# A gated linear attention and a routed expert layer in one kernel: a later start of the emptied rows, two squares on another engine, one load on another queue, and a new listed order

## The chip, the core and the metric

The kernel runs on one core of a Trainium2 chip. A core has a matrix engine (TensorE, PE in the profile; its weight loads are PEld), a vector engine (VectorE, DVE), a scalar engine for activation functions (ScalarE, ACT), a general engine (GpSimd, POOL) and SyncE (SP), which here only issues DMAs. Each engine runs its own instructions in the order in which the program lists them, and waits at an instruction until what it needs is there. SBUF is the on-chip memory, PSUM the eight banks into which TensorE writes, HBM the memory outside. The metric is the device time of one execution in microseconds (us); lower is better. All arithmetic is in float32 apart from small counting matrices.

## The reference

```python
# q, k, v, a_re, a_im: (4, 8, 768, 48)
mag = np.sqrt(a_re * a_re + a_im * a_im)
scale = np.minimum(mag, 0.999) / (mag + 1e-06)
a_re_n, a_im_n = (a_re * scale, a_im * scale)
for t in range(S):
    ar, ai = (a_re_n[:, :, t, :, None], a_im_n[:, :, t, :, None])
    new_re = ar * S_re - ai * S_im
    new_im = ar * S_im + ai * S_re
    kv = np.einsum('bhd,bhe->bhde', k[:, :, t], v[:, :, t])
    S_re, S_im = (new_re + kv, new_im)
    y[:, :, t] = np.einsum('bhd,bhde->bhe', q[:, :, t], S_re)
# bridge: x is (3072, 384)
logits = x @ w_gate                      # 8 experts
expert_idx = np.argmax(logits, axis=1)
probs = softmax(logits); gate_w = probs[arange(N), expert_idx]
for e in range(E):
    mask = expert_idx == e
    h = np.maximum(x[mask] @ w1[e], 0.0)     # 384 -> 1024
    out[mask] = gate_w[mask, None] * (h @ w2[e])
```

So there is an attention whose state decays and turns by a complex gate at each of 768 steps, and behind it a layer in which every one of 3072 tokens goes to the one of 8 experts that its router prefers. On the given inputs the experts receive 421, 406, 403, 392, 388, 370, 354 and 338 tokens.

## The kernel before

**Two stages.** In the first stage the attention is computed from the gates' logarithms and angles. It is cut into ten *units* (`UNITS`) of one batch and 128, 256 or 384 time steps; the first two units have 128 and 256 steps. For each unit `front(u)` does the elementwise work, on tiles of 128 partitions by 3 x T. In its order: ScalarE takes Ln of the real part `a` and its reciprocal by Exp (`c`); the imaginary part is multiplied by `c` (L213, on VectorE for unit 0 and on GpSimd for all others); ScalarE squares this (L334), squares the square into `junk` with a running sum (L382), and takes Ln(1 + c); VectorE adds half of it to `a` (L385); ScalarE takes an Exp with a small offset; VectorE cuts `a` at a maximum (L389) and makes three running sums `D` of it (L391, a scan from SBUF); ScalarE takes Exp(D) and Exp(-D), with which q (on GpSimd, on VectorE in unit 0) and k are multiplied (L213). For the angle, ScalarE takes an Arctan, VectorE three running sums `si` (L402, a scan with one operand in PSUM) and three instructions that bring the angle into one turn (L407, L408, L410), ScalarE a sine and a cosine. Four products (L213, into `hz` and `zp`) give q and k turned. DMAs (L429) bring these from the layout by partition into the layout by head.

Ln and Exp are in one table of ScalarE, Arctan and Sin in another, so ScalarE loads a table (L691) at each change between them.

`chunk(b, c)` then does 128 steps of one batch on TensorE: a transpose of k (L458), scores (L466), the masked scores times v (L485), the state's part (L478), the new state (L493), and a product with the constant `turn` that puts out 384 values of the token and the router's logits (L501). VectorE masks the scores (`am`, L213). ScalarE copies the other results out of PSUM. `route` finds expert and place of each token and writes its row with an indirect DMA (L560) into `xs_hbm`, which has 480 places for each expert.

**The empty places.** Not all of the 480 places get a token. Before any token is written, three DMAs (L673) write a constant row with the token number 2^20 into the upper places of all experts: from place `MINC` on. The final scatter leaves such rows out. At the end of the router the kernel compares the counts with `MINC` and the capacities (`counts_ok`); if an expert has fewer than `MINC` tokens, a slow path (from L856) does everything again.

**The order.** All work of the first stage is collected as 980 numbered operations (`P.add`), and then issued in the order of a list that is written out in the program, `ORDER`. The list sets the order on every engine and on each DMA queue. Of the numbers, 0 to 45 are `front(0)`, 62 to 107 `front(1)`; 0 and 1 are the two loads of unit 0's gates, 2 and 3 of its k and q, 62 to 65 the same for unit 1; 46 loads the first v. Number 7 is the square of unit 0, 68 and 69 are unit 1's product on GpSimd and its square. The second stage is ordered by a planner inside the program, from its own operations.

**The second stage.** The experts are run one after the other, the fullest first, each as two layers of matmuls (L815 and L834) with the outputs scattered to HBM (L755). Part of the fullest expert, its first 288 places, starts before the last tokens are routed (`early_layer`, L633).

**Setup.** `setup()` loads `wgr`, the router's weights, 28 KB, as the first DMA on SyncE's queue (L640), and GpSimd builds the constant `turn` from it (L648).

Of the kernel before, what the change touches and what calls it, by code (L numbers as in the profile page):

```python
# [15 lines left out]
ACT = mybir.ActivationFunctionType  # L16
# [14 lines left out]
CAP = 480  # L31
# [5 lines left out]
W = XW + 2  # L37
XR = 9
EARLY = 9
FAR = 4096.0  # L40
MINC = 256
ROUTES = [((0, C),)] * (B - 1) + [((0, 3), (3, 5), (5, 6))]
TB = 8
CEN = 42.0
# [6 lines left out]


ORDER = [int(i) for i in (
    "0 1 62 63 2 4 3 5 46 6 64 7 65 8 294 9 185 66 10 11 67 12 14 13 15 16 68 21 23 22 24 17 26 142 25 69 27 28 70 20 141 71 18 72 19 83 30 29 31 33 32 144 "
    "34 73 38 84 36 145 74 35 76 146 45 143 75 37 43 77 44 40 78 86 147 79 85 39 80 87 251 41 42 88 148 81 49 89 149 90 150 82 47 50 53 151 250 92 55 54 91 "
    "51 93 162 56 94 95 99 97 152 96 100 106 163 254 102 107 103 153 255 104 154 108 105 52 156 101 48 98 57 58 155 253 252 157 256 159 164 165 60 158 166 "
    "346 59 167 115 257 160 258 117 168 259 169 109 260 111 271 116 161 131 170 112 171 119 174 345 110 113 175 125 127 261 172 181 182 114 173 348 126 118 "
    "61 184 121 349 262 176 179 265 350 347 264 178 120 129 177 122 263 123 130 183 273 351 267 133 132 137 268 266 274 124 270 128 135 138 180 272 134 352 "
    "389 275 136 458 353 276 139 457 277 354 192 278 190 140 355 194 193 280 186 269 188 279 196 281 208 366 282 187 191 202 189 198 285 283 288 356 286 "
    "204 284 287 203 206 460 461 195 205 292 357 462 291 218 290 359 197 293 360 199 200 289 207 459 358 210 201 209 463 363 214 367 362 219 212 369 220 "  # L60
    "215 365 464 368 211 302 465 370 221 550 361 304 364 466 549 300 303 305 213 371 298 216 372 222 478 373 223 217 301 224 374 467 319 501 375 378 317 "
    "315 318 376 299 333 225 309 316 552 377 226 468 320 313 383 310 306 469 380 227 335 314 382 471 553 381 329 379 325 330 554 472 385 307 388 326 331 "
    "470 308 384 336 555 334 387 321 475 332 386 323 473 551 481 474 341 480 556 477 311 479 557 322 482 228 665 229 392 230 236 312 237 238 476 558 664 "
    "390 239 231 394 393 324 396 483 395 484 337 570 338 397 339 485 391 412 593 559 340 486 406 327 413 407 490 408 487 491 424 342 328 402 573 499 500 "
    "488 668 343 497 498 409 669 410 667 398 489 411 400 403 571 670 494 560 399 495 418 425 401 492 572 344 493 414 419 561 666 671 709 415 562 404 672 "
    "240 563 416 673 422 564 575 417 496 566 674 426 567 506 241 569 242 428 243 574 232 508 233 507 234 565 423 675 521 509 427 235 522 568 708 244 523 "
    "429 763 537 576 245 502 504 685 577 249 676 503 246 579 513 505 524 247 405 580 519 578 248 420 581 514 538 517 421 583 510 584 518 511 587 533 582 "
    "585 529 586 712 687 297 713 430 591 688 534 714 592 512 539 588 520 431 589 686 525 530 715 590 540 526 711 716 690 527 296 717 545 689 691 528 535 "
    "692 295 678 541 839 729 536 710 693 515 432 677 546 542 433 516 543 434 435 694 443 531 885 444 679 596 544 445 449 532 718 602 597 598 680 682 603 "
    "594 719 547 683 681 446 695 612 595 548 697 610 599 600 611 720 436 841 606 437 684 438 601 613 614 607 604 447 615 448 450 616 439 605 440 721 838 "  # L70
    "622 696 617 618 700 623 441 699 723 442 842 620 451 702 843 698 619 701 628 621 452 722 706 626 629 707 725 844 724 704 731 630 726 728 705 627 608 "
    "845 703 732 846 840 632 730 456 609 631 847 727 624 752 633 453 848 625 734 634 455 733 735 859 768 736 454 770 769 738 783 771 784 764 739 785 737 "
    "740 765 799 766 786 745 775 742 743 849 746 767 635 779 744 800 636 801 741 776 780 781 861 748 753 860 795 749 782 791 796 750 850 853 747 797 792 "
    "637 638 751 644 639 645 646 807 851 852 650 855 647 640 641 862 772 856 858 651 773 648 863 649 658 642 774 864 890 643 857 654 886 891 787 865 887 "
    "866 656 789 802 808 902 798 892 653 659 660 663 888 867 661 893 903 657 906 871 868 898 662 907 872 655 754 869 880 788 870 878 777 652 790 889 876 "
    "803 854 778 874 804 873 882 899 793 881 875 805 794 914 879 806 755 809 756 758 894 810 877 811 895 812 915 757 813 819 904 820 884 821 825 908 759 "
    "905 814 815 822 909 896 883 823 826 938 897 816 817 824 818 762 900 829 760 761 910 901 939 828 912 911 827 936 913 916 937 830 917 940 831 832 918 "
    "919 920 941 926 921 927 942 928 922 923 929 943 932 924 833 925 930 944 931 933 935 834 835 836 945 837 946 934 947 948 954 969 949 955 956 950 951 "
    "952 960 953 957 970 963 961 958 975 964 959 962 965 976 971 966 967 972 979 977 968 973 978 974 "
).split()]  # L80


# [117 lines left out]
def gateloop_then_moe(ctx, tc, gates, qk, v, wg, w1, w2, out):  # L200
# [8 lines left out]
    def bc(ap, shape):  # L209
        return ap.to_broadcast(shape)  # L210
# [83 lines left out]
    with ExitStack() as att:  # L294
# [55 lines left out]
        def front(u):  # L350
# [27 lines left out]
            activ(a, a, ACT.Ln, (A,), (A,), "LE", n)  # L378
            activ(c, a, ACT.Exp, (A,), (Ck,), "LE", n, scale=-1.0)
            mul(pool, n, im, im, c, (Bk, Ck), (Bk,))  # L380
            activ(c, im, ACT.Square, (Bk,), (Ck,), None, n)
            P.add("ACT", act_t(n) + 0.1, lambda: nc.scalar.activation(junk[:, :, sl], c, func=ACT.Square, accum_out=chk[:, u:u + 1]),  # L382
                  (Ck,), ("junk", ("chk", u)))
            activ(c, c, ACT.Ln, (Ck,), (Ck,), "LE", n, bias=one)
# [252 lines left out]
            P.add("seam", 7.0, lambda: None, tuple(("rows", B - 1, c) for c in range(C)), ("seam",))  # L637

        def setup():
            nc.sync.dma_start(wgr, wg)  # L640

            def sel():
                nc.gpsimd.memset(turn, 0.0)
                for p in range(4):
                    for j in range(2):
                        nc.gpsimd.tensor_copy(turn[64 * j:64 * j + 64, p, 48 * j:48 * j + 48],
                                              ident[64 * j:64 * j + 64, 64 * j:64 * j + 48])
                nc.gpsimd.tensor_copy(turn[:, :, 96:104], wgr[:, 0:32].rearrange("p (a e) -> p a e", a=4))  # L648
            sel()
            for t in sb:  # L650
                nc.gpsimd.memset(t[96:128], 0.0)

        setup()
        with tc.manual_schedule():
            for u in range(NU):
                if u < NU - 2:
                    front(u)
                b, t0, t1 = UNITS[u]
                if u == NU - 3:
                    front(NU - 2)  # L660
                    early_rows()
                if u == NU - 2:
                    front(NU - 1)
                    early_rest()
                for z, x in (((0, 1), (0, 2)), ((1, 0), (1, 1), (1, 2)))[u] if u < 2 else ():
                    P.add("POOL", 1.2, lambda z=z, x=x: nc.gpsimd.memset(padding(z, x), 0.0),
                          (), (("zero", z, x),), after=moved[u][:1])
                if t0 % TU == 0:
                    load_v(b, t0 // TU)
                if u == 3:  # L670
                    for h in range(3):
                        h0, h1 = MINC + 64 * h, (MINC + 64, MINC + 128, CAP)[h]
                        P.add("SP", 0.65, lambda h0=h0, h1=h1: nc.sync.dma_start(  # L673
                            xs_hbm.rearrange("(e s) w -> s e w", e=E)[h0:h1],
                            bc(empty[0:h1 - h0, None, :], [h1 - h0, E, W])), (), (("empty", h),), lat=2, wire=3.7, after=moved[1])
                for c in range(t0 // 128, t1 // 128):
                    chunk(b, c)
                    for r0, r1 in ROUTES[b]:
                        if r1 == c + 1:
                            route(b, r0, r1)  # L680
                            if b == B - 2:
                                fullest()
                            if b == B - 1 and r1 == 3:
                                ranks()
            early_layer()
            assert sorted(ORDER) == list(range(len(P.ops)))
            for i in ORDER:
                o = P.ops[i]
                if o["tag"] and o["tag"] != getattr(P, "cur", None):
                    P.cur = o["tag"]  # L690
                    nc.scalar.preload_act_table_set("natural_log_exp_and_others" if P.cur == "LE" else "trig_and_small")  # L691
                o["fn"]()
# [314 lines left out]
```

## Time and profile before

| what | value |
|---|---|
| median of 3 runs | 518.16 us (516.49 to 522.58) |
| the profiled execution | 518.39 us, span of its records 516.7 us |
| busy over the span | PE 449.3, PEld 317.7, DVE 259.9, ACT 203.5, POOL 113.8 us |
| first matmul | at 30.14 us |
| first stage's VectorE work mostly done | at about 220 us |
| first matmul of the expert layer (L633) | at 239.37 us |
| DMA | 82.65 MB, mean 160 GB/s |
| PE clock granted, mean | 0.964 |

The profiled execution took 1.7 us more than the span, which is the time around the records. In the first stage VectorE is busy almost without a break, in the second TensorE. In a view by windows, each engine's column gives the busy time in that stretch and, in brackets, how many instructions; a granted clock below 1.00 is TensorE running slower than it could.

### The profile page before, as it was taken

Reading aid. Unit: us, or ns where it says so; the run is one execution under the profiler, and the core shown is the slowest. Engines: PE = TensorE matmul, PEld = TensorE weight load, DVE = VectorE, ACT = ScalarE, POOL = GpSimd, SP = SyncE. Lnnn points to the kernel's source line nnn. Section 1 sums busy time; section 2 is a strip of 40 time slices with the busy share of each in tenths; the row PEclk is TensorE's granted clock in tenths of the full one; section 3 lists DMA queues with packets and bytes.
Section 4 is the critical chain, followed back from the end, with each engine's and each line's share of the span. In section 5 each row is a group of like instructions: output and inputs, shape, how many; then the busy total and the mean of one; then the engine's idle time right before and its main releaser. Section 6 shows DMA issues by size and latency. Waiting matters only on the chain. (4 is left out here: it accounts for less than half of the span.)

```text
span 516.7 us, 7202 instructions
## 1 busy us (share of the span) xinstructions
PE 449.3 (87%) x2739; PEld 317.7 (61%) x2739; DVE 259.9 (50%) x432; ACT 203.5 (39%) x297; POOL 113.8 (22%) x126
## 2 busy tenths in 40 slices
PE   0056679897979799999899999999999999999995
PEld 0046568787869688997585554455555455555553
DVE  5899999999989879944022311212111012110101
ACT  6996977979979747642110000000010000000000
POOL 7254032222271352523001000010200201010102
PEclk9997779998989979999999999999999999999998
DMA  8857487675788975475897940672403160000001
GB/s 258 227 164 235 115 250 221 182 228 184 183 246 248 243 221 148 136 238 202 247 309 172 355 122 15 177 272 96 120 0 122 47 259 21 15 30 14 30 1 45
DMA packets 46074, 82.65 MB, mean 160 GB/s; under 512 B 20961, under 2 KB 36988, under 8 KB 43121
## 3 DMA queue, kind: packets, MB, share of 16 engines
q1 hardware_dynamic: 41872, 71.88, 48.0%
q0 software_dynamic: 3200, 9.86, 5.2%
q10 hardware_dynamic: 960, 0.39, 0.3%
q8 instruction: 23, 0.38, 0.3%
q14 instruction: 19, 0.15, 0.1%
HBM read 53.93 MB, written 13.24 MB: 130 GB/s over the span
## 5 line engine op out<-in xcount | busy, mean ns | idle before, releaser
L466 PE MATMUL bank<-hz 128*128 128x128 f32 (+1 forms) x384 | 58.6, 303 | 39.2 <-DMA hz<-zp 31.3
L815 PE MATMUL bank<-Z,hz 128*128 128x416 f32 (+2 forms) x240 | 84.4, 507 | 0.0
L466 PEld LDWEIGHTS bank<-hz 128*128 128x128 f32 (+1 forms) x384 | 51.4, 209 | 43.7 <-DVE cs L407 30.1
L755 POOL DMA_INDIRECT out_dram<-yo,gi x24 | 23.6, 984 | 240.4 <-DVE yo L766 183.9
L821 ACT ACTIVATE ht<-bank 128x416 f32<-128x416 f32 (+2 forms) x20 | 10.2, 512 | 152.6 <-PE bank L815 152.6
L815 PEld LDWEIGHTS bank<-Z,hz 128*128 128x128 f32 x240 | 45.5, 190 | 36.1 <-issue 21.8
L834 PE MATMUL bank<-hz,ht 128*128 128x384 f32 (+1 forms) x176 | 59.3, 488 | 0.0
L766 DVE TENSOR_SCALAR yo<-bank,gi 128x384 f32<-128x384 f32 x24 | 14.7, 616 | 80.2 <-PE bank L834 74.1
L818 DVE TENSOR_SCALAR ht<-bank 128x416 f32<-128x416 f32 (+2 forms) x20 | 11.7, 584 | 72.9 <-PE bank L815 72.9
L834 PEld LDWEIGHTS bank<-hz,ht 128*128 128x128 f32 (+1 forms) x176 | 30.3, 175 | 20.4 <-issue 2.9
L815 PE MATMUL bank<-Z,w1first 128*128 128x192 f32 (+2 forms) x144 | 41.0, 441 | 0.0
L213 POOL TENSOR_TENSOR AB<-AB,C 128x1152 f32<-128x1152 f32 (+2 forms) x9 | 22.7, 2520 | 79.1 <-ACT C L334 62.2
L834 PE MATMUL bank<-w2b,ht 128*128 128x384 f32 (+1 forms) x128 | 37.6, 488 | 0.0
L834 PE MATMUL bank<-w2b,zp 128*128 128x384 f32 (+1 forms) x112 | 37.4, 486 | 0.0
L493 PE MATMUL bank<-v,kt 128*96 128x48 f32 x320 | 32.8, 259 | 4.9 <-ACT kt L460 4.9
L485 PE MATMUL bank<-am,v 128*48 128x128 f32 x384 | 31.3, 298 | 6.0 <-DVE am L213 6.0
L213 DVE TENSOR_TENSOR am<-bank,causal 128x512 f32<-128x512 f32 x48 | 32.1, 676 | 8.4 <-PE bank L466 7.8
L493 PEld LDWEIGHTS bank<-v,kt 128*96 128x96 f32 x320 | 31.3, 176 | 6.7 <-ACT kt L460 5.4
L391 DVE TENSOR_TENSOR_SCAN D<-AB,lend,C 128x384 f32<-128x384 f32 (+2 forms) x30 | 35.0, 1200 | 0.2
L815 PEld LDWEIGHTS bank<-Z,w1first 128*128 128x128 f32 x144 | 26.1, 190 | 14.5 <-issue 7.3
L560 POOL DMA_INDIRECT xs_hbm<-xg,slot x24 | 28.8, 1199 | 27.7 <-ACT yt L489 9.9
L821 ACT ACTIVATE zp<-bank 128x192 f32<-128x192 f32 (+2 forms) x12 | 5.4, 446 | 72.7 <-PE bank L815 72.7
(141 smaller groups left out, 680.1 us busy)
## 6 DMA issues: line engine op xcount, KB each, us to landing
hz<-in_w_dram SPq DMA_DIRECT2D x9, 1536.0 KB, 8.1
AB<-in_gates_dram SPq DMA_DIRECT2D x12, 576.0 KB, 4.4
Z<-in_qk_dram SPq DMA_DIRECT2D x12, 576.0 KB, 5.5
w2b<-in_w_dram SPq DMA_DIRECT2D x4, 1536.0 KB, 12.0
hz<-zp SPq DMA_DIRECT2D x12, 432.0 KB, 4.8
v<-in_v_dram SPq DMA_DIRECT2D x8, 576.0 KB, 6.6
w1first<-in_w_dram SPq DMA_DIRECT2D x3, 1536.0 KB, 6.3
hz<-hz SPq DMA_DIRECT2D x6, 432.0 KB, 8.2
```

What stands on the lines that cost most here:

```text
L213: (eng or nc.vector).tensor_tensor(out=o, in0=a, in1=b, op=op)
L391: P.add("DVE", 2 * T * 0.00105 + 0.19, lambda g=g: nc.vector.tensor_tensor_scan(d[:, g, :], a[:, g, :], c[:, g, :], lend[:, b, g, c0:c0 + ...
L466: nc.tensor.matmul(SC[hf][:, (h % 4) * 128:(h % 4) * 128 + 128], lhsT=hk[0:r, h], rhs=hq[0:r, h], start=True, stop=True)
L485: nc.tensor.matmul(YT[ps, (h // 2) * 128:(h // 2) * 128 + 128], lhsT=V[:, cl, h * D:h * D + D], rhs=am[2 * par + hf][:, h % 4, :], start=( ...
L493: nc.tensor.matmul(ST[0:96, h * D:h * D + D], lhsT=kt[par][:, h * 96:h * 96 + 96], rhs=V[:, cl, h * D:h * D + D], start=(c == 0 and h == 0 ...
L560: i = nc.gpsimd.indirect_dma_start(out=xs_hbm[:, :], out_offset=bass.IndirectOffsetOnAxis(ap=R[slot][:, c:c + 1], axis=0), in_=xg[:, (g0 + ...
L755: i = nc.gpsimd.indirect_dma_start(out=out[:, :], out_offset=bass.IndirectOffsetOnAxis(ap=index, axis=0), in_=y, in_offset=None, bounds_ch ...
L766: M.add("DVE", 0.62, lambda: nc.vector.tensor_scalar_mul(yo[yi], OB[ob][:, 0:DM], gate), (("O", ob),) + reads, (("yo", yi),))
L815: nc.tensor.matmul(HB[hb][:, 0:n - n0], lhsT=w1b[e % NW][:, c:c + 128], rhs=xrt[s][:, d, n0:n], start=(d == 0), stop=(d == DT - 1))
L818: M.add("DVE", 0.6, lambda f_=f_, hb=hb: nc.vector.tensor_scalar_max(ht[h][:, f_, n0:n], HB[hb][:, 0:n - n0], 0.0), (("H", hb),), (("ht", ...
L821: M.add("ACT", 0.6, lambda f_=f_, hb=hb: nc.scalar.activation(ht[h][:, f_, n0:n], HB[hb][:, 0:n - n0], func=ACT.Relu), (("H", hb),), (("ht ...
L834: nc.tensor.matmul(OB[ob][p0:p0 + m, 0:DM], lhsT=ht[t % NH][:, f_, c0:c0 + m], rhs=w2b[t % NV][:, f_ * DM:f_ * DM + DM], start=(f_ == 0), ...
```

## The change

Four things change.

1. `MINC` is 288 instead of 256, and the three DMAs of empty rows write 64 places each of the 8 experts (before: 64, 64 and 96).
2. The square of units 0 and 1 (number 7 and 69) is a VectorE product of the tile with itself instead of a ScalarE activation.
3. `wgr` is loaded by a DMA on ScalarE's queue instead of SyncE's.
4. `ORDER` is another list of the same 980 numbers.

```diff
-MINC = 256
+MINC = 288
...
 ORDER = [int(i) for i in (
-    "0 1 62 63 2 4 3 5 46 6 64 7 65 8 294 9 185 66 10 11 67 12 14 13 15 16 68 21 23 22 24 17 26 142 25 69 27 28 70 20 141 71 18 72 19 83 30 29 31 33 32 144 "
+    "0 62 3 1 46 4 63 5 2 66 294 65 67 6 64 7 185 8 9 10 68 21 22 24 69 11 12 70 13 14 71 15 16 23 18 25 26 142 17 27 20 28 141 19 83 72 30 29 31 33 32 144 "
...
             mul(pool, n, im, im, c, (Bk, Ck), (Bk,))
-            activ(c, im, ACT.Square, (Bk,), (Ck,), None, n)
+            if u < 2:
+                mul("DVE", n, c, im, im, (Bk,), (Ck,))
+            else:
+                activ(c, im, ACT.Square, (Bk,), (Ck,), None, n)
...
         def setup():
-            nc.sync.dma_start(wgr, wg)
+            nc.scalar.dma_start(wgr, wg)
...
-                        h0, h1 = MINC + 64 * h, (MINC + 64, MINC + 128, CAP)[h]
+                        h0, h1 = MINC + 64 * h, MINC + 64 * h + 64
                         P.add("SP", 0.65, lambda h0=h0, h1=h1: nc.sync.dma_start(
                             xs_hbm.rearrange("(e s) w -> s e w", e=E)[h0:h1],
-                            bc(empty[0:h1 - h0, None, :], [h1 - h0, E, W])), (), (("empty", h),), lat=2, wire=3.7, after=moved[1])
+                            bc(empty[0:h1 - h0, None, :], [h1 - h0, E, W])), (), (("empty", h),), lat=2, wire=3.0, after=moved[1])
```

In the new list SyncE's first loads are: unit 0's real gates, unit 1's real gates, one of unit 0's q and k, unit 0's imaginary gates, the first v, unit 1's imaginary gates, the other of unit 0's q and k. Before they were both gates of unit 0, both of unit 1, then q and k, then v. On ScalarE, unit 1's Ln and Exp now stand directly behind unit 0's. On VectorE, two of unit 0's angle scans (L402) and then unit 1's square stand ahead of unit 0's cut (L389) and its scans (L391). From about the third unit on the two lists differ by exchanges of neighbours: masks, router steps, angle scans and DMAs swap places within a few positions. The three DMAs of empty rows stay among the same loads of the seventh unit, two of them now ahead of a load of q or k that they stood behind. The operations of the second stage and their order are the same.

## The prediction

> **What bounds the kernel now.** I read the windows first, since the page's shares are means over two unlike stages. Columns: length of the window, then busy time (instructions) of each engine, granted clock, DMA share, GB/s.
>
> ```profile
> core 0: us, PE busy (x) PEld busy (x) DVE busy (x) ACT busy (x) POOL busy (x), PEclk, DMA share, GB/s
> 0.00:10.00 10.00, 0.00 (x0) 0.00 (x0) 3.70 (x9) 6.01 (x10) 6.59 (x38) 1.00 0.76 229
> 10.00:20.00 10.00, 0.00 (x0) 0.00 (x0) 8.11 (x16) 9.85 (x14) 4.42 (x11) 1.00 0.95 301
> 20.00:30.00 10.00, 0.00 (x0) 0.00 (x0) 9.86 (x15) 8.68 (x10) 5.25 (x3) 1.00 0.73 188
> ...
> 120.00:140.00 20.00, 19.45 (x211) 17.93 (x210) 19.83 (x24) 18.55 (x26) 3.34 (x1) 0.91 0.64 181
> ...
> 220.00:240.00 20.00, 18.86 (x221) 16.94 (x218) 9.64 (x46) 7.60 (x15) 4.85 (x7) 1.00 0.80 258
> ...
> 300.00:400.00 100.00, 100.00 (x344) 54.11 (x343) 19.04 (x41) 6.31 (x12) 7.87 (x8) 1.00 0.37 110
> ```
>
> VectorE idles 6.3 + 1.9 = 8.2 us in the first 20, then hardly at all to 220 (the waits of VectorE name 9 us there, the longest 3.08 us on L466). TensorE then has a backlog of some 19 us to 239, and nothing but matmuls to 512. So the end is set by: when VectorE's first-stage list gets going, how much it loses on the way to 220, and fixed TensorE work behind it. None of the four edits touches an operation behind 239.4. All the gain or loss must show in the start of L633, now at 239.37.
>
> The losses on the way are no waits by name. They are long instructions. The groups by shape show the same scan at two prices:
>
> ```profile
> L391 DVE TENSOR_TENSOR_SCAN D<-AB,lend,C 128x384 f32<-128x384 f32 x18 | 26.6, 1514 | 0.2
> L402 DVE TENSOR_TENSOR_SCAN cs<-bank,tend,AB 128x384 f32<-128x384 f32 x18 | 17.6, 998 | 0.2
> ```
>
> The timeline says why:
>
> ```profile
> 10.24 1.84 POOL L213 TENSOR_TENSOR AB<-AB,C 128x768 f32<-128x768 f32 x1 [2.47 <-ACT C L334]
> 10.33 2.41 DVE L391 TENSOR_TENSOR_SCAN D<-AB,lend,C 128x128 f32<-128x128 f32 x2
> 12.14 2.26 POOL L666 MEMSET hz<- 32x1280 f32 x2
> 12.77 1.66 DVE L373 COPY lend<-D 128x3 f32<-128x3 f32 x1
> ...
> 19.73 0.56 DVE L213 TENSOR_TENSOR hz<-Z,cs 128x384 f32<-128x384 f32 x1 [1.74 <-ACT cs L334]
> ```
>
> Two scans of 0.47 us take 2.41 beside a GpSimd product, a 0.15 us copy takes 1.66 beside GpSimd's memsets and ends with them. A GpSimd product that meets angle scans (L402) or masks, whose data lie in PSUM, costs VectorE nothing. Summed over the shapes against their undisturbed rows: D scans 9.0 us, L213 k products 2.7, zp products 2.2, lend copies 3.7, a count 2.1: about 20 us lost.
>
> **The change, part by part.**
>
> *Router's operand to ScalarE's queue.* Its issue took 0.39 us and SyncE's next began at 1.26, it at 0.81: all first loads move up 0.45 us. ScalarE's queue pays an issue (0.60 to 0.72 us in its L429 rows) ahead of a table load that took 1.28 us; it would end near 2.8 and ScalarE waited for its data until 4.49. L648 needs the operand at 7.08; it landed in 1.9. Cost nothing.
>
> *Loads in the new order.* Unit 0's real gates were issued at 1.26 and landed 3.2 later, at 4.46; now near 4.0. The imaginary gates were second, 0.39 MB with what is ahead, landed 1.73 + 3.4 = 5.1; unit 1's were fourth, 1.18 MB, landed 2.79 + 5.3 = 8.1. Now unit 0's are fourth with 0.98 MB: 5.1 + 3.0 x 0.59/0.79 = 7.3, less 0.45, is **6.9**. So the product that ran at 5.60 starts 1.3 later. Unit 1's imaginary gates are sixth, 1.97 MB: between 8.1 and v's 4.38 + 6.6 = 11.0 (2.16 MB), 10.4 less 0.45, is 10.0.
>
> *Squares.* ScalarE loses 0.52 and 0.83 us, VectorE gains 0.56 (a 384 product) and 0.95 (a 768 product), 1.51 us, where it idles 8.2. Unit 1's Ln and Exp, 1.7 us, now run while ScalarE waits for the late product. From the product at 6.9: product and square 1.2, so ScalarE's checksum at 8.1; it and Ln to 9.3; table, Arctan, table (1.30, 0.54, 1.29) to 12.5; Exp to 13.1. Then the cut L389 and three scans, 1.8, to 14.9, while ScalarE does unit 1's checksum and Ln. Behind the scans VectorE has a copy, a scan, a copy, L407, L408, two products, L410 and unit 1's L385: 4.3 us, to 19.2; ScalarE in the same time has two Exps, a table, Arctan and cosine, to 18.7. The row above reads 19.73: **0.5 us early**.
>
> [...] Unit 1's GpSimd product would run 10.0 to 11.85, its memsets (1.13 each) to 13.0 and 14.15. The cut, a tensor_scalar wanted at 13.1, falls just inside the second: 1.05 us more on the chain, first hz product at 20.3, **0.6 late**. [...] I take the nearest row, the blocked copy: +0.6. The old lend copy's 1.5 us loss is gone, but lay under ScalarE's table load. Also queued behind the new square of unit 1, which waits for GpSimd (11.85), are this cut and the scans; they wait for ScalarE until 13.1, which covers it by 0.2 us. If the load is 1 us later, 0.8 shows.
>
> *Empty rows.* 32 x 8 x 1672 B = 0.43 MB less, 1.6 us at the 274 GB/s of the window 159 to 168, in which they are issued; there DMA is 0.94 busy, but TensorE's waits on DMA are 0.2 us (171.0) and VectorE's are on ScalarE and TensorE. Two of them now go ahead of k's load (issued at 166.5, k's product follows at about 193): 2 issues and 1.7 MB, some 6 us, covered. I take -0.2, and 0 to -1.6 as the ends. Counts are all at least 338, so the slow path is not taken.
>
> *The list after 20 us.* The same instructions, exchanged by a few places. Near unit 2, GpSimd's product (24.69) meets the third D scan or, as before, the copy behind it. ScalarE's first L429 DMA now stands ahead of unit 2's Ln and waits for VectorE's last zp product: Ln and Exp start about 0.6 us later than ScalarE would be free, so the product comes during the last scan, as before. At 181 two 0.17 us router steps go behind a mask that TensorE waited 2.52 us for: -0.3. Elsewhere, what meets what cannot be read from the list, since VectorE runs later than the list assumes. One met or missed product is worth 2.1 (D scans of 5.07 to 5.16 against 2.95) to 2.45 (k product of 3.80 against 1.35). Of the 13 products to 145 us five met nothing (27.5, 69.1, 93.25 in the main, 117.06, 133.38). I bound the exchanges at two more or two fewer of them, -5 to +5, and take -0.1.
>
> **Sum.** +0.6 - 0.2 - 0.3 - 0.1 = 0 on L633, against the profiled 518.39 (span 516.7 and 1.7 around it). That execution stands 0.2 above the median of 518.16; I forecast **518.2**.
>
> **Rivals.**
>
> *Forecast, no change:* between 515.5 and 521; 1% (5.2 us) is about what a measurement of this kernel tells from no change. For it: VectorE's sum is the same, and what is freed lies at 0 to 20. Chance 0.62.
>
> *Faster, fewer collisions and warmer TensorE:* the list frees two more products (-4.9) and the stall at 181 (2.52, after which the clock was 0.53 from 185 to 190 and VectorE waited 3.08) goes. -4.9 - 3 gives 510.3. Against it: most neighbours of products are the same. A smaller one, the early branch of the cut and all empties' time (-1.1 - 1.4), gives 515.7 and is part of the first case. Chance over 1%: 0.16.
>
> *Slower, products that were free meet SBUF work:* place: the q products at 69.1, 93.25, 117.06, and the product at 133.38, now beside angle scans and masks. The new list puts router steps and lend copies of SBUF data near three of them. Each blocked costs about 2.4; the point is three lost, from which TensorE also starves: 3 x 2.4 gives **525.4**. For it: the rows at 48.48 and 142.55 (2.30 us for a count of 8 numbers). Against it: TensorE's own backlog takes the last ones. Chance over 1%: 0.22.
>
> *The change doesn't do what it says:* a square on VectorE gives ScalarE nothing because ScalarE waits for the load anyway: the 6.9 above is already that. 518.8; in the first case.
>
> **Range.** 512 to 525: the first case and most of both others. Its own is 515.5 to 521.
>
> **What would show it.** Product of unit 0 near 6.9; L389 of unit 0 at 13.1 or 14.15; first hz product 19.2 to 20.3; D scans' mean still near 1.5 us; L633 at 239.4. Wrong if L633 moves by over 3 us, or if the time moves without it.

## The result, and the profile after

| | before | changed |
|---|---|---|
| median | 520.63 us (9 runs, 516.49 to 523.41) | 525.78 us (9 runs, 521.65 to 526.60) |
| profiled execution | 518.39 us, span 516.7 | 525.95 us, span 524.2 |
| mean clock granted to TensorE | 0.964 | 0.952 |

The changed kernel is **slower by 1.0%**: ratio 1.0098, 95% interval 1.0069 to 1.0128. The forecast was 518.2 us in a range of 512 to 525. It stood on the first three runs of before (518.16); over nine runs the median is 520.63. The profiled pair differs by 7.5 us, more than the medians (5.1), because the profiled execution of before was one of its faster ones.

Of the runs below, the profile of e6 is of a disturbed execution, so that no station of it is compared with others.

All lines of the changed kernel stand 3 lower in the file: L633 is now L636, L834 is L837, L466 is L469, L391 is L394, L691 is L694. These windows answer to the first view of the prediction.

```profile
core 0: us, PE busy (x) PEld busy (x) DVE busy (x) ACT busy (x) POOL busy (x), PEclk, DMA share, GB/s
0.00:10.00 10.00, 0.00 (x0) 0.00 (x0) 3.54 (x6) 5.69 (x9) 6.29 (x38) 1.00 0.81 250
10.00:20.00 10.00, 0.00 (x0) 0.00 (x0) 8.62 (x22) 9.70 (x14) 4.54 (x11) 1.00 0.78 242
20.00:30.00 10.00, 0.00 (x0) 0.00 (x0) 9.82 (x14) 6.25 (x7) 5.23 (x3) 1.00 0.89 222
120.00:140.00 20.00, 17.47 (x171) 16.55 (x171) 17.63 (x25) 16.80 (x24) 3.05 (x2) 0.83 0.47 136
```

Two rows matter. Between 20 and 30 us ScalarE is busy 6.25 us, before 8.68. Between 120 and 140 VectorE and TensorE are **both** busy 2 us less than before (19.83 and 19.45), at a lower clock (0.83, before 0.91). Two engines that each idle while the other has work wait for each other. The groups by shape, on the other hand, show the scans at the prices of before:

```profile
L394 DVE TENSOR_TENSOR_SCAN D<-AB,lend,C 128x384 f32<-128x384 f32 x18 | 26.4, 1516 | 0.2
L405 DVE TENSOR_TENSOR_SCAN cs<-bank,tend,AB 128x384 f32<-128x384 f32 x18 | 17.8, 1001 | 0.2
```

So what GpSimd's products cost these scans has not changed. Laid beside each other, the timelines show where the time went (start of each in us; the L388 of a unit is before's L385):

| | before | changed | late by |
|---|---|---|---|
| first `hz` product of unit 0 | 19.73 | 19.08 | -0.65 |
| D scans (L391, now L394) of the third unit | 40.6 | 41.0 | 0.4 |
| L388, fifth unit | 75.1 | 75.6 | 0.5 |
| L388, eighth unit | 140.9 | 144.8 | 3.9 |
| L388, tenth unit | 196.6 | 201.6 | 5.0 |
| first matmul of the early layer (L636) | 239.37 | 243.53 | 4.2 |
| first L837 | 252.82 | 260.19 | 7.4 |
| end | 516.7 | 524.2 | 7.5 |

Two places make it: some 3.5 us between 75 and 145 us, and 3.2 us in the **seam**, as I call the stretch from L636 to the first L837 (13.45 us before, 16.66 now). Behind the seam nothing differs (263.9 and 264.0 us to the end).

**The first place.** From the fifth unit's L388 to the eighth's, before and then changed:

```profile
75.06:140.90 65.84, 58.56 (x614) 52.62 (x612) 65.22 (x75) 58.43 (x78) 14.56 (x5) 0.96 0.71 204
75.57:144.84 69.27, 60.62 (x613) 55.26 (x611) 65.35 (x74) 58.06 (x77) 14.71 (x5) 0.91 0.65 188
```

VectorE is busy for 65.22 us and for 65.35: its work takes as long as it did. Its idle time has grown from 0.62 to 3.92 us, and that is the whole loss of this place. VectorE's timeline in the changed kernel, and then TensorE's; the bracket is the idle time ahead of the row and what ended it.

```profile
110.90 5.16 DVE L394 TENSOR_TENSOR_SCAN D<-AB,lend,C 128x384 f32<-128x384 f32 x3
...
120.53 1.01 DVE L405 TENSOR_TENSOR_SCAN cs<-bank,tend,AB 128x384 f32<-128x384 f32 x1
...
121.65 0.68 DVE L213 TENSOR_TENSOR am<-bank,causal 128x512 f32<-128x512 f32 x1
...
124.50 0.69 DVE L213 TENSOR_TENSOR am<-bank,causal 128x512 f32<-128x512 f32 x1 [0.91 <-PE bank L469]
...
130.38 0.69 DVE L213 TENSOR_TENSOR am<-bank,causal 128x512 f32<-128x512 f32 x1 [0.88 <-PE bank L488]
```

```profile
94.23 1.59 PE L469 MATMUL bank<-hz 128*128 128x128 f32 x8 [3.93 <-DVE am L213]
...
122.39 2.08 PE L469 MATMUL bank<-hz 128*128 128x128 f32 x8 [3.42 <-DVE am L213]
```

TensorE idles 3.42 us for a mask that VectorE comes to at 121.65, behind angle scans and router steps. Then its eight score matmuls take 2.08 us instead of 1.16, at half clock (0.50 granted from 122.39 to 124.47 us). Now VectorE waits for TensorE, at 124.50 for these scores and at 130.38 for a product of masked scores and v (L488) that comes late behind them. Before, TensorE's longest idle in this stretch was for the router:

```profile
117.35 1.13 PE L466 MATMUL bank<-hz 96*128 96x128 f32 x8 [0.96 <-DMA hz<-zp]
120.53 0.18 PE L542 MATMUL bank<-oh,before 128*128 128x48 bf16 x1 [1.72 <-DVE oh L213]
```

Behind this idle, too, the clock fell (0.50 from 122 to 124 us), but no wait of VectorE followed. So half clock alone does not make the loss.

**The seam.** ScalarE's rows (ACTq is the issue of a DMA in its queue) and TensorE's, before:

```profile
244.15 0.41 ACT L635 ACTIVATE zp<-bank 128x288 f32<-128x288 f32 x1 [1.04 <-PE bank L633]
247.42 0.42 ACTq L784 DMA_DIRECT2D AB<-xs_hbm  x1
247.88 0.41 ACT L635 ACTIVATE zp<-bank 128x288 f32<-128x288 f32 x1 [3.33 <-DMA xs_hbm<-xg,slot]
```

```profile
248.35 4.63 PE L633 MATMUL bank<-Z,w1first 128*128 128x288 f32 x18 [1.33 <-ACT zp L635]
```

and in the changed kernel:

```profile
246.85 0.41 ACT L638 ACTIVATE zp<-bank 128x288 f32<-128x288 f32 x1 [1.18 <-PE bank L636]
251.18 0.37 ACTq L787 DMA_DIRECT2D AB<-xs_hbm  x1
251.59 0.41 ACT L638 ACTIVATE zp<-bank 128x288 f32<-128x288 f32 x1 [4.33 <-DMA xs_hbm<-xg,slot]
```

```profile
252.06 7.63 PE L636 MATMUL bank<-Z,w1first 128*128 128x288 f32 x24 [2.33 <-ACT zp L638]
```

A load of the first expert's remaining tokens stands in ScalarE's queue and waits for the last scatter of rows. Whatever stands behind it on ScalarE waits too (the evacuation at 251.59, for 4.33 us). Before, three evacuations of the early layer stood ahead of it, now only two, so TensorE runs out of free banks one matmul group earlier: 2.33 us of idle instead of 1.33, and then 24 matmuls in 7.63 us, at a granted clock of 0.50 from 252.06 to 253.50 us and 0.66 to 256.00, where they take 6.09 us in e9. Another 0.5 us is a wait of the first L837 for the last evacuation.

### The profile page after: what moved, and what is told of

It reads as the page before. It is cut to its first block, busy times and chain, and to the rows that moved or that the text cites. A ratio compares the mean times of both kernels' runs of the same rounds, so it can differ in the third digit from the quotient of the medians.

```text
span 524.2 us, 7203 instructions
## 1 busy us (share of the span) xinstructions
PE 452.5 (86%) x2739; PEld 321.0 (61%) x2739; DVE 259.6 (50%) x434; ACT 202.3 (39%) x295; POOL 111.4 (21%) x126
## 5 line engine op out<-in xcount | busy, mean ns | idle before, releaser
L469 PE MATMUL bank<-hz 128*128 128x128 f32 (+1 forms) x384 | 61.7, 313 | 40.6 <-DMA hz<-zp 32.9
L469 PEld LDWEIGHTS bank<-hz 128*128 128x128 f32 (+1 forms) x384 | 54.2, 219 | 44.7 <-DVE cs L411 30.7
L837 PE MATMUL bank<-hz,ht 128*128 128x384 f32 (+1 forms) x176 | 59.3, 488 | 0.0
L837 PEld LDWEIGHTS bank<-hz,ht 128*128 128x128 f32 (+1 forms) x176 | 30.3, 175 | 20.4 <-issue 2.9
L837 PE MATMUL bank<-w2b,ht 128*128 128x384 f32 (+1 forms) x128 | 37.6, 488 | 0.0
L837 PE MATMUL bank<-w2b,zp 128*128 128x384 f32 (+1 forms) x112 | 37.4, 486 | 0.0
L496 PE MATMUL bank<-v,kt 128*96 128x48 f32 x320 | 31.6, 253 | 6.4 <-ACT kt L463 6.4
L488 PE MATMUL bank<-am,v 128*48 128x128 f32 x384 | 31.0, 298 | 6.8 <-DVE am L213 6.8
L496 PEld LDWEIGHTS bank<-v,kt 128*96 128x96 f32 x320 | 30.0, 170 | 8.0 <-ACT kt L463 6.7
L394 DVE TENSOR_TENSOR_SCAN D<-AB,lend,C 128x384 f32<-128x384 f32 (+2 forms) x30 | 33.2, 1149 | 0.3
```

The lines of the kernel that those rows point to most:

```text
L394: P.add("DVE", 2 * T * 0.00105 + 0.19, lambda g=g: nc.vector.tensor_tensor_scan(d[:, g, :], a[:, g, :], c[:, g, :], lend[:, b, g, c0:c0 + ...
L469: nc.tensor.matmul(SC[hf][:, (h % 4) * 128:(h % 4) * 128 + 128], lhsT=hk[0:r, h], rhs=hq[0:r, h], start=True, stop=True)
L488: nc.tensor.matmul(YT[ps, (h // 2) * 128:(h // 2) * 128 + 128], lhsT=V[:, cl, h * D:h * D + D], rhs=am[2 * par + hf][:, h % 4, :], start=( ...
L496: nc.tensor.matmul(ST[0:96, h * D:h * D + D], lhsT=kt[par][:, h * 96:h * 96 + 96], rhs=V[:, cl, h * D:h * D + D], start=(c == 0 and h == 0 ...
L837: nc.tensor.matmul(OB[ob][p0:p0 + m, 0:DM], lhsT=ht[t % NH][:, f_, c0:c0 + m], rhs=w2b[t % NV][:, f_ * DM:f_ * DM + DM], start=(f_ == 0), ...
```

## The experiments

"Places" are places in `ORDER`; at the cuts used here the same numbers stand ahead of the cut in both lists. Ratios are to the kernel before in the same group of runs, with 95% intervals. Its median was 520.9 us for e1 to e4, 526.1 for e5 to e8, 525.2 for e9 to e12, 526.4 for e13 to e16 and 520.3 for e17 and e18. In the three groups in between nearly all kernels were later between the tenth L388 and L636 (45 to 49 us instead of 41 to 46). All twelve profiles of these groups show one stop that the others don't have: somewhere between 215 and 230 us VectorE stands for 3.6 to 5.2 us, released by an event that names no instruction of this core ("remote" in the profile), and ScalarE stands for 4.2 to 5.1 us at the same time. That is about as much as before's median is later there. What causes the stop is open; so stations are compared within a group, or as distances that lie ahead of it.

| run | what | ratio | L388, 5th to 8th unit | clock, 120 to 130 us | seam |
|---|---|---|---|---|---|
| (before) | | | 65.8 | 0.83 | 13.45 |
| (changed) | | 1.0098 (1.0069 to 1.0128) | 69.3 | 0.66 | 16.66 |
| e1 | edits, old list | 1.0013 (0.9988 to 1.0039) | 65.9 | 1.00 | 13.23 |
| e2 | new list, no edits | 1.0091 (1.0053 to 1.0129) | 68.4 | 0.83 | 19.17 |
| e3 | changed, old tail | 1.0008 (0.9977 to 1.0039) | 69.3 | 0.66 | 13.35 |
| e4 | changed, old 242 to 480 | 0.9993 (0.9968 to 1.0018) | 65.7 | 1.00 | 14.64 |
| e5, e16 | both places old | 0.9942 (0.9912 to 0.9972), 0.9982 (0.9951 to 1.0013) | 66.2, 66.0 | 1.00 | 13.53 |
| e6 | two masks moved | 1.0029 (0.9996 to 1.0061) | | | |
| e7 | changed, loads on SyncE | 1.0002 (0.9975 to 1.0028) | 67.6 | 0.75 | 12.98 |
| e8, e17 | both old, loads on SyncE | 0.9939 (0.9908 to 0.9970), 0.9970 (0.9936 to 1.0003) | 68.5, 67.9 | 1.00 | 12.31, 11.85 |
| e9 | changed, again | 1.0057 (1.0026 to 1.0088) | 69.8 | 0.66 | 15.08 |
| e10 | one mask moved | 1.0076 (1.0029 to 1.0123) | 68.8 | 0.66 | 15.78 |
| e11 | changed, old 302 to 480 | 1.0031 (0.9999 to 1.0063) | 65.5 | 1.00 | 15.87 |
| e12 | new start, old rest | 1.0007 (0.9980 to 1.0034) | 65.8 | 0.83 | 13.88 |
| e13 | first half of 302 to 480 old | 1.0160 (1.0108 to 1.0212), of 4 runs | 69.3 | 0.66 | 15.26 |
| e14 | second half old | 1.0060 (1.0028 to 1.0092) | 67.7 | 0.72 | 14.85 |
| e15 | new to 241, old rest | 1.0005 (0.9981 to 1.0029) | 66.5 | 1.00 | 13.71 |
| e18 | before, loads on SyncE | 0.9961 (0.9934 to 0.9988) | 65.9 | 0.83 | 11.85 |

### The list or the edits

```diff
 # e1: the changed kernel
-ORDER = new
+ORDER = old
 # e2: the kernel before
-ORDER = old
+ORDER = new
```

> The three small edits of the change (288, squares on VectorE, the router's operand on ScalarE's queue), with the list of before. Theory A (the loss is in the list): as before, 520.6 us within 1 and a ratio of 0.998 to 1.002; L636 starts near 239.4 and the early layer takes 13.4 us to the first L837. Rival B (the edits cost it, by the order of DMAs at the start or by VectorE's 1.5 us more): near 525, L636 near 243.

> The kernel before with the new list and none of the three edits. Theory A (list): 525 to 527 us, ratio near 1.010, L633 near 243.5, the early layer 16.7 us to the first L834; the start is slower than in the changed kernel, since ScalarE has the squares back, by 0.5 us. Rival B (edits): 520.6. A third case, the list needs the edits: over 528.

The loss is in the list: e1 is level with before, e2 as slow as the changed kernel. Both profiles say something on the start, too. In e1 the edits make the fifth unit's L388 2.0 us late (77.1), yet the tenth is late by 0.2 (196.7) and L636 by 1.1. In e2 the D scans of the third unit come at 43.4, 2.5 us behind the changed kernel, and the ratio is no worse. **Two microseconds at the start are not two at the end.** The seam of e2 was longer than I expected: the profiled execution took 531.1 us, TensorE idled 3.29 us there and half clock followed for some 6 us.

### The two places

```diff
 # e3, e4, e5 (and e16): the changed kernel
-ORDER = new
+ORDER = new[:947] + old[947:]                              # e3
+ORDER = new[:242] + old[242:481] + new[481:]               # e4
+ORDER = new[:242] + old[242:481] + new[481:947] + old[947:]  # e5, e16
```

> The changed kernel with the last 33 numbers of the list as before, so that three evacuations of the early layer instead of two stand ahead of ScalarE's token load. Theory C (the seam is lost at that load, which stands in ScalarE's queue and waits for the last scatter): L636 near 243.5 as in the changed kernel, but 13.5 instead of 16.7 us from there to the first L837; time 522.6, 3.2 below the changed kernel. Rival D (the seam is slow because the last scatter and the clock come later, whatever stands where): 16 to 17 us again, 525.8.

> The changed kernel with places 242 to 480 of the list as before (the same numbers stand there in both lists): about 80 to 137 us of the run. Theory E (the stage loses its 4 us where the masks and the last steps of the first router change places): VectorE's D scan that starts at 142.1 in the changed kernel and 137.4 before starts at 138.5, L636 near 240.5, the seam still 16.7, time 522.5. Rival F (the loss is spread over the list or comes from the start): D scan at 141 or later, L636 at 243, 525.8.

> The changed kernel with both places 242 to 480 and the last 33 of the list as before; the new start and all three edits stay. Theory G (the seam loses more, the longer TensorE idles there, since its clock halves behind an idle of 2.33 us and not behind 1.86, so that either old part alone already gives back nearly all): no more than the two alone gave, 519.5 to 521, seam 13.4, L636 near 239.4. Rival H (two separate losses of some 5 us each, as the medians of the two alone suggest if they are added): 516.

> Old places 242 to 480 and old tail in the changed kernel, once more on another chip: 0.994 again (0.991 to 0.997) if the gain is the kernel's; 1.000 if it was the chip's.

The tail does what theory C says: L636 at 243.69, as late as in the changed kernel, but a seam of 13.35. TensorE's row in e3:

```profile
252.57 4.63 PE L636 MATMUL bank<-Z,w1first 128*128 128x288 f32 x18 [1.23 <-ACT zp L638]
```

The middle does what theory E says, and more: the seventh unit's D scan, at 142.1 in the changed kernel, comes at 136.9 (137.4 before), L636 at 239.4. I had expected the seam to stay at 16.7; it was 14.64, as TensorE idled 1.86 us there and no half clock followed.

Each part alone returned all that the medians show, which cannot be added up; with both the ratio was 0.9942 once and 0.9982 in another group. The two intervals share 0.9951 to 0.9972. Theory H (0.991) falls, theory G's 0.998 to 1.000 fits the second only. That the seam's stall and half clock come on top of the lateness explains part of it (e4's seam is 2.0 us shorter with the same tail); the rest lies within the intervals. The seam of 13.53 in e5 and e16, as forecast, is in part chance: no evacuation waits in either profile, but TensorE waits 0.90 and 1.42 us for the weights (`w1first`) and then takes 3.15 and 2.88 us for its first six matmuls, which take 1.69 in the changed kernel.

### The queue of the seam

```diff
-if e == 0:
-    M.add("ACT", 0.5, lambda: which.update(...), ...)
...
-eng, dma, wh = ("ACT", nc.scalar, "ACT") if e == 0 and i % 2 else ("SP", nc.sync, e)
+eng, dma, wh = ("SP", nc.sync, e)
 # e7: changed kernel; e8, e17: with the list of e5; e18: kernel before
```

The two lines above the load go with it: they fetch the expert's number on ScalarE, which nothing there needs any more.

> The changed kernel with its own list, and the first expert's two token loads on SyncE's queue instead of ScalarE's; everything else stands in the same order on every engine. Theory C (the seam waits because an evacuation stands behind a load in ScalarE's queue): no idle of TensorE over 1 us in the early layer and full clock, 12.2 to 12.7 us from L636 to the first L837, L636 near 243.5, time 521.5. Rival K (the loads land later through one queue and the matmuls behind the early layer wait for them, or the wait is for the scatter in another way): seam under 13, but as much lost by 275, time 525 or more.

> Old middle, old tail and the token loads on SyncE's queue, with the new start and the three edits. By theory C the seam has no idle of TensorE, 12.2 to 12.7 us, 1 us less than before; L636 near 239.4; time 519 to 519.8, ratio 0.996 to 0.999. Rival K: 521 or more.

> Old places 242 to 480, old tail, and the first expert's two token loads on SyncE's queue, with the new start and the three edits, once more beside before: had 0.994 once, while the same without the moved loads had 0.994 and then 0.998. If the version is better than before by the 1.1 us that the seam saves and by 1 to 2 us of the list: 0.994 to 0.997. If the first was the chip's: 0.998 to 1.000.

> The kernel before, with nothing changed but the first expert's two token loads on SyncE's queue. Theory C (an evacuation stands behind the load on ScalarE): the 1.1 to 1.3 us of TensorE's idle in the early layer go, 12.2 to 12.7 us instead of 13.4 from L633 to the first L834, ratio 0.997 to 0.998. Rival K (given back behind it): 1.000.

No evacuation waits any more, whatever the list. TensorE in e18:

```profile
240.57 10.43 PE L633 MATMUL bank<-Z,w1first 128*128 128x288 f32 x42
250.84 10.48 PE L832 MATMUL bank<-hz,zp 128*128 128x384 f32 x32
```

There is no bracket in the first row: 42 matmuls without a wait, a seam of 11.85 us, 1.6 less than before. In all four runs the time from the first L834 (here under other line numbers) to the end is 263.7 to 263.9 us, so nothing is given back: rival K falls. **e18 is 0.4% faster than before** with this one edit: 0.9961. The version with all three, e8 and e17, is not told from it; in e17 VectorE comes 2.2 us later to the fifth unit's cut than in e16 with the same list (86.3, 84.1). The traces show the wait: at 75 TensorE waits 1.75 us in e8 and 2.92 in e17 for a DMA (`hz<-hz`), and VectorE then 1.62 and 2.60 us for the scores behind it. That is ahead of places 302 to 480; why the DMA is late is open.

### What in the middle

```diff
 # e6: the changed kernel
-... 304 371 303 ... 222 305 374 ...    ... 332 323 479 ... 394 336 665 ...
+... 304 305 371 303 ... 222 374 ...    ... 332 336 323 479 ... 394 665 ...
 # e10: the changed kernel
-... 359 ... 361 ... 367 ... 219 ... 209 ...
+... 359 209 ... 361 ... 367 ... 219 ...
```

> The changed kernel with two numbers of the list moved: the mask 305 stands directly behind its scores 304 again, the mask 336 directly behind the mask 332; nothing else. Theory I (late masks: VectorE does angle scans and router steps before two masks, TensorE idles 3.93 us at 94.2 and 3.42 at 122.4, comes back at half clock, and then VectorE waits for it): both idles under 1.5 us, the D scan of 142.1 at 138.5, L636 at 240.5, time 521.3 as with the whole old middle. Rival J (the 4 us are in other exchanges of the middle, such as the order of the chunks on TensorE or what meets a GpSimd product): D scan at 141 or later, time over 524.5.

> The changed kernel once more, beside the others of this group: ratio 1.010 again (1.006 to 1.013), L636 4 us later than L633 in the first profile of before, the seam 16 to 17 us.

> The changed kernel with one number of the list moved: the mask 209 stands directly behind the three D scans of its unit again, ahead of the lend copy, an angle scan and the mask 219. Theory L (this one exchange begins the loss: TensorE idles 3.93 us for that mask at 94.2, comes back at half clock, its later scores are late, and VectorE waits): the idle falls to 2.1 us, the D scan of 110.9 starts at 110 and that of 142.1 at 139.5, ratio 1.004 to 1.006. Rival M (the second idle, at 122.4, costs it alone): 142.1 stays within 1, ratio 1.009 to 1.010.

e6 was a miss. Its profile shows which waits there are: TensorE's idle of 3.92 us at 94.4 is still there (that mask was another, 209), and the one at 122.4 has become a wait of 2.75 us for ScalarE's copy of k (L463). Its ratio of 1.0029 (0.9996 to 1.0061) leaves room for theory I's 1.001 and not for rival J's 1.007, but it isn't told from that of the changed kernel in e9 either (1.0057), and theory I had put both idles under 1.5 us. So it shows neither. e10 then moved mask 209, and TensorE's rows show that the first idle shrinks and its half clock goes:

```profile
92.76 1.16 PE L469 MATMUL bank<-hz 128*128 128x128 f32 x8 [2.20 <-DVE am L213]
...
121.99 2.06 PE L469 MATMUL bank<-hz 128*128 128x128 f32 x8 [3.22 <-DVE am L213]
```

But the second idle stays, the distance of the two L388 falls by 1.0 us only (69.8 in e9, 68.8), and the ratio is no better than that of e9. Theory L falls as the main cause: between the first and the second idle VectorE of the changed kernel has no wait longer than 0.34 us. (e9 itself shows that the changed kernel's loss varies: 1.0098 and 1.0057, with overlapping intervals. Its L636, at 248.5, is 9 and not 4 us later than L633 in the first profile, with the delay of its group in it. In its seam TensorE idled 2.30 us, and no half clock followed.)

```diff
 # e11, e13, e14: the changed kernel; a = the 90 numbers at old[302:392], b = those at new[302:392]
-ORDER = new
+ORDER = new[:302] + old[302:481] + new[481:]                              # e11
+ORDER = new[:302] + a + [x for x in new[302:481] if x not in a] + new[481:]  # e13
+ORDER = new[:302] + b + [x for x in old[302:481] if x not in b] + new[481:]  # e14
 # e12, e15: the changed kernel
+ORDER = new[:140] + old[140:]                                             # e12
+ORDER = new[:242] + old[242:]                                             # e15
```

> The changed kernel with places 302 to 480 of the list as before, so that the first idle (94.2) stays and what leads to the second (122.4) goes. Theory L: the D scan of 142.1 at 141, ratio 1.006 to 1.009. Rival M: 138.5, ratio 1.000 to 1.002. Both in equal parts: 139.8, 1.004.

> The changed kernel with the 90 operations that stood first in places 302 to 480 of the list before put first again in their old order; the other 89 of these places follow in the new order. Measure: the time from VectorE's L388 of the fifth unit to that of the eighth, 65.5 to 66.2 us in five of the six runs with all of 302 to 480 old that have been looked at for it, 67.6 to 70.9 with the new ones. Theory P (it is lost ahead of 118 us, where masks stand behind angle scans and router steps): 66 to 67. Theory Q (it is lost behind that, where TensorE takes the scores of the other half first and the router's counting matmul late): 69 to 70.

> The complement: the 90 operations that stand first in places 302 to 480 of the new list stay first in the new order, the other 89 follow in the order of before. Theory P: 69 to 70 us between the two L388. Theory Q: 66 to 67. If the two halves only cost it together (a mask late and then scores in the other order): under 67 in both.

> The three edits with the first 140 places of the new list and everything behind them as before. If the new start is worth its 0.65 us at the first hz product but loses it at the two DMAs on ScalarE's queue, as the trace of the changed kernel shows, then 0.999 to 1.001. If old middle and old tail gained their 0.6% over before by the new start alone: 0.994.

> The three edits with places 0 to 241 of the new list and everything behind as before. Old middle and tail in an otherwise new list had a ratio of 0.994, new start and old rest 1.001. If the new places 140 to 241 bring the 0.6%, then 0.994; if the new places 481 to 946 do, or if it was the spread between chips, 1.000.

e11 settles the block: 65.5 us between the two L388, the D scan at 136.4, where rival M had put 138.5 (its ratio is 1.0031 because the new tail, 15.87 us of seam, is still in; my numbers for M had left that out). In all, the runs with 302 to 480 as before have 65.5 to 66.5 us there, but for the 67.9 and 68.5 told above; those with the new ones 67.6 to 69.8. VectorE's idle time tells the two kinds apart without overlap: from the sixth unit's cut (L392, at 106 to 113 us) to the eighth L388 it is 0.35 or 0.55 us in all eleven profiles with 302 to 480 as before, and 1.2 to 2.7 us in the six with the new ones. The windows from 120 to 130 us of the changed kernel and of e11 show the same difference:

```profile
120.00:130.00 10.00, 7.47 (x54) 6.94 (x56) 8.43 (x14) 7.47 (x11) 0.06 (x1) 0.66 0.39 131
```

```profile
120.00:130.00 10.00, 8.98 (x101) 8.61 (x99) 9.93 (x11) 9.41 (x14) 0.00 (x0) 1.00 0.44 148
```

101 matmuls against 54, VectorE busy 9.93 against 8.43. Of the halves, neither brings the distance under 67: with the first half old it is 69.3 (2.29 us of that idle), with the second old 67.7 (1.03 us of it; another 2.9 us of idle lie ahead, behind a DMA that TensorE waits 2.31 us for at 76), where TensorE has a new wait for VectorE, and half clock behind it:

```profile
121.17 2.05 PE L469 MATMUL bank<-hz 96*128 96x128 f32 x8 [3.73 <-DVE cs L405]
```

So the second half carries more, but none of the exchanges undone singly (e6, e10) gives it back. In it TensorE takes a transpose and its scores (410, 412) ahead of those that stood first before (390, 392), and VectorE's masks follow that order. That the orders of the two engines must fit together is how I read it; e13's ratio of 1.016 would agree, but comes from 4 runs. Which exchange starts it stays open.

e12 and e15 say that the new start and the new places up to 241 are worth nothing that can be measured (1.0007 and 1.0005).

## Why the prediction was wrong, by its own steps

**The start came nearly as worked out.** VectorE and GpSimd in the changed kernel:

```profile
7.02 0.56 DVE L213 TENSOR_TENSOR AB<-AB,C 128x384 f32<-128x384 f32 x1 [3.71 <-DMA AB<-in_gates_dram]
...
12.48 0.96 DVE L213 TENSOR_TENSOR C<-AB 128x768 f32<-128x768 f32 x1 [0.23 <-POOL AB L213]
13.36 0.59 DVE L392 TENSOR_SCALAR AB<-AB 128x384 f32<-128x384 f32 x1
...
19.08 0.56 DVE L213 TENSOR_TENSOR hz<-Z,cs 128x384 f32<-128x384 f32 x1
```

```profile
12.51 1.16 POOL L669 MEMSET hz<- 32x1280 f32 x1
13.61 1.31 POOL L669 MEMSET hz<- 32x1280 f32 x1
```

The product at 6.9 came at 7.02, the square of unit 1 cost 0.96, the first `hz` product at 19.2 came at 19.08. At the fork between 0.5 us early (no wait) and 0.6 late (the cut waits out a memset) the wait came, but a short one. The prediction had GpSimd's product from 10.0 on and the cut inside the second memset. The product began at 10.65, so the cut, at 13.36, fell into the end of the first: it took 0.59 us instead of 0.43, ended 0.28 us behind that memset, and the second memset took 1.31 us instead of 1.16. In e16 and e17, which have the same start and a product from 10.0 on, the cut does wait out the second memset, which ends at 14.10 in e17, and the first `hz` product comes at 19.5:

```profile
13.03 1.35 DVE L392 TENSOR_SCALAR AB<-AB 128x384 f32<-128x384 f32 x1 [0.22 <-ACT C L334]
```

In all sixteen profiles in which this cut meets a memset, it ends 0.28 or 0.29 us behind the end of one. Before, its row lies clear of the memsets (at 9.40, the first memset at 12.14), so the +0.6 stood on the row of the blocked copy (1.66 us). That the cut waits, too, is what the traces of the changed kernel and of e17 show, in which it takes 0.59 and 1.35 us instead of 0.43; the place of the memsets was wrong. A larger cut waits for one of GpSimd's products in the same way, in e17 (2.91 us, where that of e16 below takes 0.75):

```profile
86.33 2.91 DVE L392 TENSOR_SCALAR AB<-AB 128x1152 f32<-128x1152 f32 x1
89.28 2.84 DVE L394 TENSOR_TENSOR_SCAN D<-AB,lend,C 128x384 f32<-128x384 f32 x3
```

```profile
86.00 2.62 POOL L213 TENSOR_TENSOR AB<-AB,C 128x1152 f32<-128x1152 f32 x1 [14.68 <-DMA hz<-hz]
```

and in e16, where the cut was done when the product began (at 85.00), the scans pay instead:

```profile
84.12 0.75 DVE L392 TENSOR_SCALAR AB<-AB 128x1152 f32<-128x1152 f32 x1
84.91 5.16 DVE L394 TENSOR_TENSOR_SCAN D<-AB,lend,C 128x384 f32<-128x384 f32 x3
```

Cut and scans together are 5.75 and 5.91 us: the loss moves, it doesn't change.

**"So the product comes during the last scan, as before" failed.** The product came at 24.71, when it did before (24.69), but VectorE was earlier: its scans ended at 24.51. The copy behind them took 0.17 us instead of 2.40, and three later instructions beside GpSimd's work took 2.6 us more than before (at 26.04, 27.98 and 30.95). The step also looked at unit 2's Ln and Exp, and not at the square behind them. ScalarE in the changed kernel, then before:

```profile
28.06 1.33 ACTq L432 DMA_DIRECT2D hz<-zp  x2
29.44 1.16 ACT L334 ACTIVATE C<-AB 128x1152 f32<-128x1152 f32 x1 [3.15 <-POOL Z L213]
```

```profile
25.20 1.38 ACTq L429 DMA_DIRECT2D hz<-zp  x2
27.60 1.16 ACT L334 ACTIVATE C<-AB 128x1152 f32<-128x1152 f32 x1 [0.65 <-POOL AB L213]
```

Two DMAs stand in ScalarE's queue ahead of unit 2's square and go out at 28.06 instead of 25.20, so the square is 1.84 us late, and so is the Ln(1 + c) that unit 2's L388 waits for (33.22, before 32.97): the 0.65 us are gone. As in the seam, work of ScalarE stands behind DMAs in its queue; what these two waited for until 28.06 the trace does not name.

**The premise "when VectorE's first-stage list gets going" weighed too much.** e1 starts 2 us late and ends level. Most of the working went into the first 20 us, which e12 shows to be worth nothing here.

**The empty rows** and the router's operand were not run alone. With the squares and the old list they are e1, 1.0013.

**"I bound the exchanges at two more or two fewer of them, -5 to +5, and take -0.1" is the first mis-sized term.** In the pair it was 3.5 us between the fifth and the eighth unit, over the runs 3.2 (the medians of the two kinds of distance, 65.9 and 69.1). That lies inside the -5 to +5, but by another mechanism than the one priced, so the bound held by luck. Collisions of GpSimd's products with VectorE's scans, 26.6 us over 18 scans before and 26.4 after, cost what they did, and VectorE's busy time in the stretch is the same (65.22 and 65.35 us). What the exchanges change is how long TensorE idles for a mask, and whether half clock follows. The trace of before had that too (2.52 us of wait at 181, clock 0.53 behind it, VectorE waiting 3.08): I priced it for the gain of a rival, and not as what an exchange can bring about anywhere.

**"None of the four edits touches an operation behind 239.4" is the second, and simply wrong.** The list's last 33 places order the matmuls of the early layer, and so set how many of its evacuations stand ahead of ScalarE's load: 3.2 us in the profiled pair, and 1.2 (e4) to 5.7 (e2) more than before's 13.45 in the other profiles with the new tail and the loads on ScalarE. The prediction's own sign for being wrong, "if L633 moves by over 3 us, or if the time moves without it", was met twice, by 4.2 and by 3.2.

**The base was low.** The sum stood on 518.16, the median of three runs; nine runs give 520.63. So of the 7.6 us between the forecast and the median of 525.78, 2.4 were in the base, and the rest is what the change does.

**The rivals.** The slower one named 525.4, near to what came, but by luck: it starts from the low base, and its cause is free GpSimd products that meet SBUF work. The unchanged scans and VectorE's unchanged busy time speak against that. The range ended at 525.0, since I took the losses of one mechanism for all that can go wrong; on the right base it would have held 525.78.

## What to carry to other kernels

Where a list orders several engines, an exchange on one is priced by who waits for the instruction moved back, first of all TensorE for a mask, and by what its clock does behind the idle (here 3.42 us of idle, then eight matmuls in 2.08 us instead of 1.16), not by the work exchanged. A load or store that waits on another stage must not stand in the queue of an engine that also frees PSUM banks (here an evacuation waited 4.33 us behind one, and e18, without it, has a seam 1.6 us shorter than before): look in every ScalarE queue for what stands behind each DMA, at the seams above all. And a delay at the start is worth only what is left of it at the bottleneck's last wait (in e1, 2.0 us at the fifth unit and 0.2 at the tenth), so follow it through the stations before working on its tenths.

## What the runs showed of the hardware

TensorE's idle of 3.1 to 3.9 us in the first stage was followed by eight matmuls at 1.59 to 2.08 us instead of 1.16, in the changed kernel, e9, e10 and e14. Behind 1.23 to 1.86 us in the seam no half clock followed (e3, before, e4; 18 matmuls in 4.63 us in e3 and in before, there at a granted clock of 1.00). But shorter idles were also followed by slow matmuls elsewhere: 1.72 us at 120.53 in before (granted clock 0.50 from 122 to 124 us), and 0.90 and 1.42 us ahead of L636 in e5 and e16 (six matmuls in 3.15 and 2.88 us, in the changed kernel in 1.69). And in between it was not one thing: 2.33 us was followed by half clock in the changed kernel (24 matmuls in 7.63 us), while 2.30, 2.48, 2.54 and 2.64 us in e9, e13, e10 and e11 were not (24 matmuls in 6.09 us). So theory G's line between 1.86 and 2.33 is no threshold, and the length of the last idle alone does not decide.

Scans and cuts under the same list pay for one GpSimd product in different rows from run to run (5.75 us in e17 and 5.91 in e16, above). A timeline of one execution that shows a scan "free" does not show that the list made it so.
